# Per-step rstd on ScalarE and g folded into W1, in a kernel of sliding-window attention, LayerNorm and MLP

## Chip, cores and metric

The kernel runs on one core of a Trainium2 chip. The metric is the device time of one execution in microseconds.

The engines are TensorE (PE; its weight loads are PEld), VectorE (DVE), ScalarE (ACT), GpSimd (POOL) and SyncE (SP, which here only issues DMA). L191 is line 191 of the kernel that is spoken of. The line numbers of the two kernels differ.

## The reference, cut

```python
def _attn_ref(q, k, v):                      # 8 batches, 8 heads, 576 rows, head size 64
    ...
    rel = pos[:, None] - pos[None, :]
    mask = (rel >= 0) & (rel < 64)           # causal window of 64 rows
    scores = np.where(mask, scores, -1000000000.0)
    ...                                      # softmax
    return np.matmul(attn, v)

def _moe_ref(x, g_ln, w_ch1, w_ch2):         # x: (8, 576, 512)
    mu = np.mean(x, axis=-1, keepdims=True)
    var = np.mean((x - mu) ** 2, axis=-1, keepdims=True)
    xn = (x - mu) / np.sqrt(var + 1e-06) * g_ln
    ch = np.maximum(xn @ w_ch1, 0.0) @ w_ch2 # 512 -> 2048 -> 512
    return x + ch
```

The layer has no bias, and relu(s·a) = s·relu(a) for a positive s. So 1/sqrt(var + eps), called rstd, may be applied to each row before the first layer or only at the output. The gain g may be applied to the rows or to the rows of W1.

## The kernel before

The work is cut into nine groups of 512 rows. Groups 0 to 7 are the first 512 rows of the eight batches, and group 8 holds the last 64 rows of all eight (the tails, four blocks of two batches). While the MLP of group g runs on PE, the attention of group g+1 is computed in slots between its pieces. The schedule is written by hand: instructions of one engine run in the order of the program.

```python
    def w1_cast(i, eng):                     # W1 float32 -> float16, 128x1024 at a time
        ...
            nc.gpsimd.tensor_copy(out=dst, in_=t)

    def cast_qk(b, half):                    # q and k of a later group, on GpSimd
        ...

    def s_mask(g, j):                        # the mask is multiplied in on VectorE, in place
        pt = pts[(g, j)]
        ...
        nc.vector.tensor_tensor(out=ptv, in0=ptv, in1=mb, op=ALU.mult)

    def b_step(g, kb):                       # probabilities x values, then LayerNorm, 128 rows
        ...
        nc.vector.tensor_tensor(out=xn, in0=xps[:, :, 0:D], in1=rcp_b, op=ALU.mult)
        nc.vector.bn_stats(out=stats, in_=xn[...])
        nc.vector.bn_aggr(out=mvg[g][:, kb, :], in_=stats)
        nc.vector.scalar_tensor_tensor(      # z = (xn - mean) * g, not divided by the deviation
            out=z, in0=xn[...], scalar=mvg[g][:, kb, 0:1], in1=gB,
            op0=ALU.subtract, op1=ALU.mult)

    def group_stats(g, eng=nc.gpsimd):       # rstd of four blocks: integer guess, two Newton steps
        ...                                  # the guess on VectorE
        for _ in range(2):
            eng.tensor_tensor(out=ab, in0=rs, in1=rs, op=ALU.mult)
            eng.tensor_tensor(out=ab, in0=ab, in1=hv, op=ALU.mult)
            eng.tensor_scalar(out=ab, in0=ab, scalar1=-1.0, scalar2=1.5, op0=ALU.mult, op1=ALU.add)
            eng.tensor_tensor(out=rs, in0=rs, in1=ab, op=ALU.mult)

    def add_out(kb):                         # output = xn + rstd * ch
        nc.vector.scalar_tensor_tensor(
            out=o, in0=ch[kb], scalar=rstd[g][:, kb:kb + 1], in1=x_norm[(g, kb)][...],
            op0=ALU.mult, op1=ALU.add)
    ...
        if g > 0:
            at(4 if g == 1 else 0, group_stats, g)   # slot 0 of its own group
        ...
            at(2 + 6 * j, s_mask, b, j)              # slot 2: first mask product of group g+1
            ...
            at(e + 8, cast_qk, n, 0)                 # casts of group g+2, on the same GpSimd queue
```

The softmax here doesn't subtract the row's maximum and nothing guards it: scores larger than these inputs give would overflow.

## Time and profile before

| | before |
|---|---|
| time, median of 3 runs (lowest to highest) | 329.69 us (328.72 to 329.92) |
| span of the profiled run | 328.5 us |
| first Relu of group 2, an end mark of the prologue | 100.39 us |
| each of groups 2 to 5 | 32.2 us |
| groups 6 and 7 together | 67.3 us |
| last W2 cast begins | 47.20 us |

The group times are distances between the first Relu of one group and that of the next, read from the timeline. (The texts count a group from its first matmul, about 1 us earlier.)

First the table of engines and the chain of waits of the page. The engine table gives busy microseconds, share of the span, and instruction count.

```profile
PE 314.1 (96%) x2711; PEld 162.6 (49%) x2711; DVE 163.8 (50%) x307; ACT 155.4 (47%) x268; POOL 126.4 (38%) x230
...
PE 66%; DMA 13%; issue 8%; POOL 5%; SPq 4%; DVE 1%; ACT 1%; POOLq 0%; ACTq 0%
```

PE is the limit. The other engines have half their time free.

Next, groups of instructions. The columns are line, engine, operation, output from input, shape, count, then busy time in us and mean ns of one, then the idle time ahead of them and what ended it.

```profile
L321 DVE SCALAR_TENSOR_TENSOR z<-xn,mvg,gB 128x512 f16<-128x512 f32 x36 | 32.6, 907 | 1.3
L396 DVE SCALAR_TENSOR_TENSOR osb<-ch,rstdg,xn 128x512 f32<-128x512 f32 x36 | 27.0, 749 | 57.5 <-PE ch L387 46.1 <-issue 9.7 <-PE ch L426 1.6
...
L292 DVE TENSOR_TENSOR pt<-pt,mask 128x1024 f16<-128x1024 f16 x28 | 19.3, 690 | 20.9 <-ACT pt L285 11.9 <-ACT pt L279 9.0
...
L191 POOL CAST w1g<-w2s 128x1024 f16<-128x1024 f32 x4 | 4.2, 1062 | 1.5 <-DMA w2s<-in_moe_w_ch_dram 1.5
L191 POOL CAST w1g<-w1s 128x1024 f16<-128x1024 f32 x4 | 4.2, 1061 | 2.8 <-DMA w1s<-in_moe_w_ch_dram 2.6
```

The eight W1 casts are 8.4 us of GpSimd. The mask product is 690 ns on average, which matters below.

Then the timeline of GpSimd in the prologue (start, duration, engine, line, operation, output from input, count, and in brackets the idle time before and who ended it):

```profile
16.60 1.04 POOL L191 CAST w1g<-w1s 128x1024 f16<-128x1024 f32 x1 [0.73 <-DMA w1s<-in_moe_w_ch_dram]
...
27.60 1.04 POOL L191 CAST w1g<-w2s 128x1024 f16<-128x1024 f32 x1 [0.72 <-DMA w2s<-in_moe_w_ch_dram]
...
47.20 1.04 POOL L201 CAST w2s<-w2s 128x1024 f16<-128x1024 f32 x1 [0.38 <-DMA w2s<-in_moe_w_ch_dram]
```

The casts wait for DMA, not the other way round: there is some slack on GpSimd here. The waits of PE show where it stood still:

```profile
PE sc L275 <- DMA tkT<-tk: 2.2, 1, 2.2
PE ch L426 <- POOL w2s L201: 1.7, 2, 1.4
```

The first is the one late transpose of tail keys in group 7, the second the W2 casts of the prologue. Each line has the total, the number of times, and the longest.

Last, a steady group, as GpSimd and then as VectorE ran it:

```profile
101.13 0.18 POOL L352 TENSOR_SCALAR rstmp<-mvg 128x4 f32<-128x4 f32 x1
...
103.07 0.61 POOL L357 TENSOR_SCALAR rstmp<-rstmp 128x4 f32<-128x4 f32 x1
103.77 0.20 POOL L358 TENSOR_TENSOR rstdg<-rstdg,rstmp 128x4 f32<-128x4 f32 x1
103.90 1.04 POOL L128 CAST qk<-qk 128x1024 f16<-128x1024 f32 x1
```

### The profile page before, as it was taken

Reading aid. Unit: us, or ns where it says so; the run is one execution under the profiler, and the core shown is the slowest. Engines: PE = TensorE matmul, PEld = TensorE weight load, DVE = VectorE, ACT = ScalarE, POOL = GpSimd, SP = SyncE. Lnnn points to the kernel's source line nnn. Section 1 sums busy time; section 2 is a strip of 40 time slices with the busy share of each in tenths; the row PEclk is TensorE's granted clock in tenths of the full one; section 3 lists DMA queues with packets and bytes.
Section 4 is the critical chain, followed back from the end, with each engine's and each line's share of the span. In section 5 each row is a group of like instructions: output and inputs, shape, how many; then the busy total and the mean of one; then the engine's idle time right before and its main releaser. Section 6 shows DMA issues by size and latency. Waiting matters only on the chain.

```text
span 328.5 us, 6688 instructions
## 1 busy us (share of the span) xinstructions
PE 314.1 (96%) x2711; PEld 162.6 (49%) x2711; DVE 163.8 (50%) x307; ACT 155.4 (47%) x268; POOL 126.4 (38%) x230
## 2 busy tenths in 40 slices
PE   7989979999999999999999999999999999799993
PEld 2566435587654545454444444454445444344441
DVE  1895564584762564266526652655257713441021
ACT  2586504487636731682178217722772276216500
POOL 7566555648416501750184018301500462212000
PEclk9999989999999999999999999999999999999998
DMA  8999999976992898289938993991390397310022
GB/s 191 284 384 268 340 266 290 282 260 138 242 254 81 163 261 220 73 153 259 224 79 148 266 211 80 138 194 64 90 198 35 86 217 163 83 65 32 2 64 64
DMA packets 119329, 56.77 MB, mean 173 GB/s; under 512 B 95777, under 2 KB 112161, under 8 KB 119298
## 3 DMA queue, kind: packets, MB, share of 16 engines
q1 hardware_dynamic: 116096, 45.62, 60.2%
q0 software_dynamic: 3200, 10.72, 11.0%
q8 instruction: 21, 0.34, 0.4%
q14 instruction: 10, 0.08, 0.1%
q10 hardware_dynamic: 2, 0.00, 0.0%
HBM read 38.80 MB, written 9.44 MB: 147 GB/s over the span
## 4 chain that ended last, share of the span: by engine, by line
PE 66%; DMA 13%; issue 8%; POOL 5%; SPq 4%; DVE 1%; ACT 1%; POOLq 0%; ACTq 0%
PE ch L387 31%; PE hps L375 22%; DMA w2s<-in_moe_w_ch_dram 4%; DMA qk<-in_q_dram 4%; PE hph L411 4%; PE xps L307 3%; PE sc L275 2%; SPq L141 2%; PE ztp L332 2%; DMA w1s<-in_moe_w_ch_dram 2%; DMA tk<-in_k_dram 2%; DMA tv<-in_v_dram 1%; PE ch L426 1%; SPq L79 1%; PE tp L217 1%
## 5 line engine op out<-in xcount | busy, mean ns | idle before, releaser
L387 PE MATMUL ch<-w2s,hrT 128*128 128x512 f16 x544 | 125.0, 379 | 0.0
L375 PE MATMUL hps<-zT,w1g 128*128 128x512 f16 x480 | 109.9, 379 | 0.0
L379 ACT ACTIVATE hrT<-hps 128x512 f16<-128x512 f32 x120 | 72.0, 600 | 41.1 <-PE hps L375 40.6
L387 PEld LDWEIGHTS <-hrT 128*128 128x128 f16 x544 | 50.8, 98 | 56.4
L375 PEld LDWEIGHTS <-w1g 128*128 128x128 f16 x480 | 45.4, 98 | 54.6 <-issue 3.1
L366 POOL DMA_DIRECT2D out_dram<-osb x32 | 17.7, 554 | 130.9 <-DVE osb L396 59.4
L335 ACT COPY zT<-ztp 128x512 f16<-128x512 f16 x36 | 21.0, 583 | 77.7 <-PE ztp L332 77.5
L396 DVE SCALAR_TENSOR_TENSOR osb<-ch,rstdg,xn 128x512 f32<-128x512 f32 x36 | 27.0, 749 | 57.5 <-PE ch L387 46.1
L310 DVE RECIPROCAL rcp<-xps 128x8 f32<-128x8 f32 x36 | 7.4, 205 | 59.8 <-PE xps L307 59.8
L321 DVE SCALAR_TENSOR_TENSOR z<-xn,mvg,gB 128x512 f16<-128x512 f32 x36 | 32.6, 907 | 1.3
L292 DVE TENSOR_TENSOR pt<-pt,mask 128x1024 f16<-128x1024 f16 x28 | 19.3, 690 | 20.9 <-ACT pt L285 11.9
L128 POOL CAST qk<-qk 128x1024 f16<-128x1024 f32 x24 | 25.3, 1068 | 6.3 <-DMA qk<-in_q_dram 3.3
L285 ACT ACTIVATE pt<-sc 128x512 f16<-128x512 f32 x40 | 21.7, 596 | 12.1 <-PE sc L275 11.4
L315 DVE BATCH_NORM_STATS2 stats<-xn 128x6 f32<-128x512 f32 x36 | 25.0, 695 | 1.2
L313 DVE TENSOR_TENSOR xn<-xps,rcp 128x512 f32<-128x512 f32 x36 | 24.9, 692 | 1.2
L411 PE MATMUL hph<-zT,w1g 128*128 128x256 f16 x192 | 23.5, 273 | 1.5 <-ACT hrT L416 0.7
L411 PEld LDWEIGHTS <-w1g 128*128 128x128 f16 x192 | 18.0, 98 | 4.4 <-issue 1.8
L416 ACT ACTIVATE hrT<-hph 128x512 f16<-128x512 f32 x24 | 14.4, 599 | 10.2 <-PE hph L411 10.0
L147 POOL CAST vA<-v 128x512 f16<-128x512 f32 (+1 forms) x14 | 16.2, 1162 | 4.9 <-DMA v<-in_v_dram 4.6
L279 ACT ACTIVATE pt<-sc 128x512 f16<-128x512 f32 x32 | 17.4, 601 | 1.0
L307 PEld LDWEIGHTS <-pt 128*64 128x64 f16 x576 | 12.2, 110 | 9.2 <-issue 5.1
L209 ACT COPY qkT<-tp 128x1024 f16<-128x1024 f16 x10 | 10.0, 1012 | 11.4 <-PE tp L217 11.0
(65 smaller groups left out, 241.1 us busy)
## 6 DMA issues: line engine op xcount, KB each, us to landing
qk<-in_q_dram SPq DMA_DIRECT2D x16, 512.0 KB, 6.4
v<-in_v_dram SPq DMA_DIRECT2D x32, 256.0 KB, 5.8
out_dram<-osb POOLq DMA_DIRECT2D x32, 256.0 KB, 3.3
w2s<-in_moe_w_ch_dram SPq DMA_DIRECT2D x12, 512.0 KB, 5.9
qk<-in_k_dram SPq DMA_DIRECT2D x8, 512.0 KB, 6.9
qk<-in_k_dram SPq DMA_DIRECT2D x16, 256.0 KB, 5.8
w1s<-in_moe_w_ch_dram SPq DMA_DIRECT2D x4, 512.0 KB, 7.0
tk<-in_k_dram SPq DMA_DIRECT2D x8, 256.0 KB, 4.8
```

The costliest lines, as they stand in the source:

```text
L128: nc.gpsimd.tensor_copy(out=dst[:, :].rearrange("p (a j) e d -> p a e j d", j=j), in_=t[:, :].rearrange("p (a e j d) -> p a e j d", e=2, j ...
L285: nc.scalar.activation(out=pt[:, par], in_=sc[par], func=AF.Exp, bias=0.0, scale=scale)
L307: nc.tensor.matmul(out=xps[64 * r:64 * r + 64, h, :D + 1], lhsT=pt[:, par, hp, r, :], rhs=rhs, start=True, stop=True)
L313: nc.vector.tensor_tensor(out=xn, in0=xps[:, :, 0:D], in1=rcp_b, op=ALU.mult)
L315: nc.vector.bn_stats(out=stats, in_=xn[:, :, :].rearrange("p h d -> p (h d)"))
L321: nc.vector.scalar_tensor_tensor(out=z, in0=xn[:, :, :].rearrange("p h d -> p (h d)"), scalar=mvg[g][:, kb, 0:1], in1=gB, op0=ALU.subtract ...
L335: nc.scalar.copy(out=dst, in_=ztp)
L375: nc.tensor.matmul(out=hps, lhsT=w1g[:, kc, 128 * hc:128 * (hc + 1)], rhs=zT[g][:, kc, :], start=(kc == 0), stop=(kc == NKC - 1),)
L379: nc.scalar.activation(out=hrT[:, hc, :], in_=hps, func=AF.Relu, bias=0.0, scale=1.0)
L387: nc.tensor.matmul(out=ch[kb], lhsT=hrT[:, hc, 128 * kb:128 * (kb + 1)], rhs=w2s[:, hc, :], start=(hc == 0), stop=(hc == NHC - 1),)
L396: nc.vector.scalar_tensor_tensor(out=o, in0=ch[kb], scalar=rstd[g][:, kb:kb + 1], in1=x_norm[(g, kb)][:, :, :].rearrange("p h d -> p (h d) ...
L411: nc.tensor.matmul(out=hps[:, e], lhsT=w1g[:, kc, 128 * hc:128 * (hc + 1)], rhs=zT[g][:, kc, 256 * half:256 * half + 256], start=(kc == 0) ...
```

## The change

The intent: rows go to layer 1 fully normalised, so the output becomes a plain add and z needs no g. Rstd comes from two one-column ScalarE activations per block, exp(-0.5·ln(var + eps)), and the Newton chain goes. The gain is multiplied into W1 where W1 is cast anyway. Two smaller parts ride along: the tail blocks are loaded and cast some slots earlier, and their value tiles alternate between two buffer tags.

```diff
-    def w1_cast(i, eng):
+    def w1_cast(i):
...
-            nc.gpsimd.tensor_copy(out=dst, in_=t)
+        for c in range(2):
+            kc = 2 * pr + c
+            nc.gpsimd.tensor_scalar(
+                out=w1g[:, kc, (HID // 4) * q2:(HID // 4) * (q2 + 1)], in0=t[:, c],
+                scalar1=g4[:, kc:kc + 1], scalar2=None, op0=ALU.mult,
+            )
...
+    def r_step(g, kb):
+        rs = p_blk.tile([128, 1], FP32, tag="rs", name=f"rs_{g}_{kb}")
+        nc.scalar.activation(out=rs, in_=mvs[(g, kb)][:, 1:2], func=AF.Ln, bias=epst, scale=1.0)
+        nc.scalar.activation(out=rs, in_=rs, func=AF.Exp, bias=0.0, scale=-0.5)
+
+    def z_step(g, kb):
...
-        nc.vector.scalar_tensor_tensor(
-            out=z, in0=xn[...], scalar=mvg[g][:, kb, 0:1], in1=gB,
+        nc.vector.tensor_scalar(
+            out=z, in0=x_norm[(g, kb)][...], scalar1=mv[:, 0:1], scalar2=rs[:, 0:1],
             op0=ALU.subtract, op1=ALU.mult,
         )
...
-    def group_stats(g, eng=nc.gpsimd):      (all of it goes)
...
-            nc.vector.scalar_tensor_tensor(
-                out=o, in0=ch[kb], scalar=rstd[g][:, kb:kb + 1], in1=x_norm[(g, kb)][...],
-                op0=ALU.mult, op1=ALU.add)
+            nc.vector.tensor_tensor(out=o, in0=ch[kb], in1=x_norm[(g, kb)][...], op=ALU.add)
...
+    nc.scalar.preload_act_table_set("natural_log_exp_and_others")   # one set for Ln and Exp
-    nc.scalar.dma_start(out=g1, in_=...)    # g as one row of 2 KB, broadcast by PE
+    nc.scalar.dma_start(out=g4, in_=...)    # g as 512 elements of 4 bytes, one column per 128 rows
...
-        vt = p_va.tile(..., tag="vA", ...)
+        vt = p_va.tile(..., tag=("vA", "vB")[i % 2], ...)
...
     TAILS = { ... }                         # loads, casts and transposes of tails in earlier slots
```

More of the change, by code (lines that the diff above doesn't have):

```diff
@@ L12 @@
 FP16 = mybir.dt.float16
-I32 = mybir.dt.int32
-RSQRT_MAGIC = float(np.frombuffer(np.uint32(0x5F3759DF).tobytes(), dtype=np.float32)[0])
 AF = mybir.ActivationFunctionType
@@ L63 @@
     mbias = p_const.tile([128, 64], FP16, tag="mbias", name="mbias")
-    magt = p_const.tile([128, 4], FP32, tag="magt", name="magt")
-    gB = p_const.tile([128, DM], FP32, tag="gB", name="gB")
+    g4 = p_const.tile([128, NKC], FP32, tag="g4", name="g4")
+    epst = p_const.tile([128, 1], FP32, tag="epst", name="epst")
     w1g = p_const.tile([128, NKC, HID], FP16, tag="w1g", name="w1g")
@@ L71 @@
     qkT, vA, vB, pts = {}, {}, {}, {}
-    x_norm, zT, mvg, zsd, rstd = {}, {}, {}, {}, {}
+    x_norm, zT, zsd, mvs, rss = {}, {}, {}, {}, {}
     def load_qk(b, half):
@@ L110, in cast_tail @@
         k16 = p_in.tile([128, 2, H, D], FP16, tag="qk16_1", name=f"tk16_{i}")
-        vt = p_va.tile([128, 2, H, D + 1], FP16, tag="vA", name=f"vt_{i}")
+        vt = p_va.tile([128, 2, H, D + 1], FP16, tag=("vA", "vB")[i % 2], name=f"vt_{i}")
         tail16[i] = (q16, k16)
@@ L182, in w1_load @@
         )
-    def w1_cast(i, eng):
+    def w1_cast(i):
         q2, pr = divmod(i, 2)
         t = wst.pop(("w1", i))
-        dst = w1g[:, 2 * pr:2 * pr + 2, (HID // 4) * q2:(HID // 4) * (q2 + 1)]
-        if eng == "act":
-            nc.scalar.copy(out=dst, in_=t)
-        else:
-            nc.gpsimd.tensor_copy(out=dst, in_=t)
+        for c in range(2):
[4 more added lines that the diff above has]
+            )
     def w2_load(i):
@@ L315, in b_step @@
         nc.vector.bn_stats(out=stats, in_=xn[:, :, :].rearrange("p h d -> p (h d)"))
-        if g not in mvg:
-            mvg[g] = p_grp.tile([128, 4, 2], FP32, tag="mvg", name=f"mvg_{g}")
-        nc.vector.bn_aggr(out=mvg[g][:, kb, :], in_=stats)
-        z = p_blk.tile([128, DM], FP16, tag="z", name=f"z_{kblk}")
+        mv = p_blk.tile([128, 2], FP32, tag="mv", name=f"mv_{kblk}")
+        nc.vector.bn_aggr(out=mv, in_=stats)
+        mvs[(g, kb)] = mv
+    def r_step(g, kb):
+        rs = p_blk.tile([128, 1], FP32, tag="rs", name=f"rs_{g}_{kb}")
+        rss[(g, kb)] = rs
+        nc.scalar.activation(out=rs, in_=mvs[(g, kb)][:, 1:2], func=AF.Ln, bias=epst, scale=1.0)
+        nc.scalar.activation(out=rs, in_=rs, func=AF.Exp, bias=0.0, scale=-0.5)
+    def z_step(g, kb):
+        mv, rs = mvs.pop((g, kb)), rss.pop((g, kb))
+        z = p_blk.tile([128, DM], FP16, tag="z", name=f"z_{g}_{kb}")
         zsd[(g, kb)] = z
-        nc.vector.scalar_tensor_tensor(
-            out=z, in0=xn[:, :, :].rearrange("p h d -> p (h d)"), scalar=mvg[g][:, kb, 0:1], in1=gB,
+        nc.vector.tensor_scalar(
+            out=z, in0=x_norm[(g, kb)][:, :, :].rearrange("p h d -> p (h d)"), scalar1=mv[:, 0:1], scalar2=rs[:, 0:1],
             op0=ALU.subtract, op1=ALU.mult,
@@ L337, in zt_step @@
             nc.vector.tensor_copy(out=dst, in_=ztp)
-    def group_stats(g, eng=nc.gpsimd):
-        rstd[g] = p_grp.tile([128, 4], FP32, tag="rstdg", name=f"rstdg_{g}")
-        rs = rstd[g]
-        mv = mvg[g]
-        tmp = p_grp.tile([128, 3, 4], FP32, tag="rstmp", name=f"rstmp_{g}")
-        ve, hv, ab = tmp[:, 0], tmp[:, 1], tmp[:, 2]
-        nc.vector.tensor_scalar(out=ve, in0=mv[:, :, 1], scalar1=EPS, scalar2=None, op0=ALU.add)
-        nc.vector.tensor_scalar(
-            out=ab.bitcast(I32), in0=ve.bitcast(I32), scalar1=1, scalar2=None,
-            op0=ALU.logical_shift_right,
-        )
-        nc.vector.tensor_tensor(out=rs[:, :].bitcast(I32), in0=magt[:, :].bitcast(I32),
-                                in1=ab.bitcast(I32), op=ALU.subtract)
-        eng.tensor_scalar(out=hv, in0=mv[:, :, 1], scalar1=0.5, scalar2=0.5 * EPS,
-                                op0=ALU.mult, op1=ALU.add)
-        for _ in range(2):
-            eng.tensor_tensor(out=ab, in0=rs, in1=rs, op=ALU.mult)
-            eng.tensor_tensor(out=ab, in0=ab, in1=hv, op=ALU.mult)
-            eng.tensor_scalar(out=ab, in0=ab, scalar1=-1.0, scalar2=1.5, op0=ALU.mult, op1=ALU.add)
-            eng.tensor_tensor(out=rs, in0=rs, in1=ab, op=ALU.mult)
     stores, cur = [], [0]
@@ L395, in add_out @@
             o = p_blk.tile([128, DM], FP32, tag="osb", name=f"osb_{g}_{kb}", bufs=4)
-            nc.vector.scalar_tensor_tensor(
-                out=o, in0=ch[kb], scalar=rstd[g][:, kb:kb + 1],
-                in1=x_norm[(g, kb)][:, :, :].rearrange("p h d -> p (h d)"), op0=ALU.mult, op1=ALU.add,
+            nc.vector.tensor_tensor(
+                out=o, in0=ch[kb], in1=x_norm[(g, kb)][:, :, :].rearrange("p h d -> p (h d)"), op=ALU.add,
             )
@@ L444, in mlp_units @@
         return units
+    nc.scalar.preload_act_table_set("natural_log_exp_and_others")
     load_qk(0, 0)
     load_v(0, 0, 2)
-    g1 = p_const.tile([1, DM], FP32, tag="g1", name="g1")
-    ones1 = p_const.tile([1, 128], FP32, tag="ones1", name="ones1")
-    nc.scalar.dma_start(out=g1, in_=bass.AP(tensor=moe_g_ln.tensor, offset=moe_g_ln.offset, ap=[[DM, 1], [1, DM]]))
+    nc.scalar.dma_start(out=g4, in_=bass.AP(tensor=moe_g_ln.tensor, offset=moe_g_ln.offset, ap=[[1, 128], [128, NKC]]))
     load_qk(0, 1)
@@ L457 @@
     nc.vector.memset(mask, 1.0)
-    nc.vector.memset(magt, RSQRT_MAGIC)
-    nc.vector.memset(ones1, 1.0)
+    nc.vector.memset(epst, EPS)
     nc.gpsimd.affine_select(
@@ L479 @@
     for i in range(8):
-        w1_cast(i, "pool")
+        w1_cast(i)
     warm = ps_mm.tile([128, 512], FP32, tag="mm", name="warm")
@@ L492 @@
     keep_clock(4)
-    gps = ps_mm.tile([128, DM], FP32, tag="mm", name="gps")
-    nc.tensor.matmul(out=gps, lhsT=ones1, rhs=g1, start=True, stop=True)
-    nc.vector.tensor_copy(out=gB, in_=gps)
     keep_clock(1)
@@ L510 @@
     vB_cur(0, 2, 0)
+    r_step(0, 0)
+    z_step(0, 0)
     t_main(0, 0, 1, 0)
@@ L517 @@
     vB_prev(0, 2, 0)
+    r_step(0, 1)
+    z_step(0, 1)
     s_mm(0, 2, True)
@@ L522 @@
     zt_step(0, 1)
+    r_step(0, 2)
+    z_step(0, 2)
     s_mm(0, 3, True)
@@ L546 @@
     TAILS = {
-        6: ((1, load_tail, 0), (6, cast_tail, 0), (8, x_tail, 0), (16, s_mm, 8, 0), (17, s_mask, 8, 0),
-            (22, b_step, 8, 0), (28, zt_step, 8, 0),
-            (14, load_tail, 1), (24, cast_tail, 1), (26, x_tail, 1), (25, load_tail, 2), (30, cast_tail, 2)),
-        7: ((6, s_mm, 8, 1), (7, s_mask, 8, 1), (12, b_step, 8, 1), (17, zt_step, 8, 1),
-            (0, x_tail, 2), (12, s_mm, 8, 2), (13, s_mask, 8, 2), (18, b_step, 8, 2), (23, zt_step, 8, 2),
-            (7, load_tail, 3), (12, cast_tail, 3), (14, x_tail, 3), (18, s_mm, 8, 3), (19, s_mask, 8, 3),
-            (24, b_step, 8, 3), (29, zt_step, 8, 3)),
+        6: ((0, load_tail, 0), (3, cast_tail, 0), (5, x_tail, 0), (10, s_mm, 8, 0), (11, s_mask, 8, 0),
+            (16, b_step, 8, 0), (22, zt_step, 8, 0),
+            (10, load_tail, 1), (14, cast_tail, 1), (18, x_tail, 1), (20, load_tail, 2), (24, cast_tail, 2),
+            (26, x_tail, 2)),
+        7: ((1, s_mm, 8, 1), (2, s_mask, 8, 1), (7, b_step, 8, 1), (12, zt_step, 8, 1),
+            (7, s_mm, 8, 2), (8, s_mask, 8, 2), (13, b_step, 8, 2), (18, zt_step, 8, 2),
+            (0, load_tail, 3), (4, cast_tail, 3), (6, x_tail, 3), (13, s_mm, 8, 3), (14, s_mask, 8, 3),
+            (19, b_step, 8, 3), (24, zt_step, 8, 3)),
     }
@@ L560, in at, with bz @@
             slots[min(i, len(slots) - 1)].append((f, a))
+        def bz(i, *p):
+            at(i, b_step, *p)
+            at(i + 1, r_step, *p)
+            at(i + 2, z_step, *p)
         b = g + 1
         if g == 0:
-            at(0, b_step, 0, 3)
+            bz(0, 0, 3)
             at(1, zt_step, 0, 2)
             at(3, zt_step, 0, 3)
-            at(4, group_stats, 0, nc.vector)
             at(11, t_main, 1, 0, 0, 1)
@@ L575 @@
             at(17, s_mm, 1, 1, True)
-            at(18, b_step, 1, 0)
-            at(21, b_step, 1, 1)
+            bz(18, 1, 0)
+            bz(21, 1, 1)
             at(22, zt_step, 1, 0)
@@ L589 @@
             at(30, cast_qk, 2, 1)
-            at(31, b_step, 1, 2)
+            bz(31, 1, 2)
         if g == 1:
             at(0, alloc_qkT, 2)
-            at(1, b_step, 1, 3)
+            bz(1, 1, 3)
             at(2, zt_step, 1, 2)
@@ L613 @@
                 at(10 + 4 * j, s_mask, 2, j)
-                at(13 + 4 * j, b_step, 2, j)
+                bz(13 + 4 * j, 2, j)
                 at(17 + 4 * j, zt_step, 2, j)
@@ L619 @@
                 at(2 + 6 * j, s_mask, b, j)
-                at(7 + 6 * j, b_step, b, j)
+                bz(7 + 6 * j, b, j)
                 at(min(13 + 6 * j, 29), zt_step, b, j)
-        if g > 0:
-            at(4 if g == 1 else 0, group_stats, g)
         for i, f, *p in TAILS.get(g, ()):
-            at(i, f, *p)
+            if f is b_step:
+                bz(i, *p)
+            else:
+                at(i, f, *p)
         if 0 < g and b + 1 < B:
```

## The prediction

> **What bounds the kernel now.** TensorE. The engine table has PE busy 314.1 of 328.5 us; the chain of waits is 66% PE. In the timeline the middle groups repeat every 32.2 us (99.43, 131.66 ... 228.40 us) with PE gapless. VectorE (50%), ScalarE (47%) and GpSimd (38%) have room, so work saved there is worth nothing by itself. PE waits in two places:
> - Prologue, 0 to 49 us. DMA is about 90% busy. In the chain, w2 loads, then their GpSimd casts, release second-layer matmuls at 46.87 us (1.38 us gap before; 0.36 us at 44.09).
> - Group 7, 260.4 to 295.6 us, about 3 us longer than its neighbours. PE waits 2.19 us at 283.04 for transposed tail keys: tail 1's casts sat on GpSimd behind output stores until 256.9, so tail 2's v load started at 259.58, tail 3's loads at 269 to 275, its casts at 278.
>
> **Costs.**
> - Removed: integer and Newton steps, about 0.5 us VectorE and 2.7 us GpSimd a group; the g broadcast (2.07 us of PE, hidden). z loses its gB operand: 907 ns (749 undisturbed) becomes perhaps 450. The output add goes from 749 to about 695 ns, as the xn multiply (692).
> - Added: 72 one-column activations. Two ScalarE forms (583 ns for 512 columns, 1012 for 1024) leave about 155 ns fixed; the Trainium skill, "ScalarE: Activation LUTs", What ACT_TABLE_LOAD costs, adds about 93 ns for a pointer operand. Estimate 0.25 + 0.2 us. The same page has Ln and Exp in one set; the built program has one table load.
> - W1 cast: 8 casts of 1024 columns (1061 ns) become 16 multiplies of 512. A 512 cast takes 617 ns; the Trainium skill, "GPSIMD Engine Reference", Engine selection, calls one-input work "roughly line-rate". I estimate 0.65 to 0.95 us each: +2 to +6 us of GpSimd. No trace yet shows this operation at that size.
> - g load: 512 four-byte packets on the busy DMA: +0.3 to 0.9 us, from 27 ns mean packet time (60.2% of 16 engines over 116096 packets).
>
> **On the critical path.**
> - Steady groups: Ln waits for the aggregate, in front of the next Relu. At 107 to 110 us: aggregate ends 109.37, Ln and Exp about 109.9, Relu about 110.5 instead of 110.25, its PSUM buffer was wanted at 110.47. Stall under 0.1 us, once a group; layer 2 has none. About +0.5 us overall.
> - Prologue: GpSimd waits 3.4 us for DMA between the w1 casts and over 2 us after them, so most of its extra is absorbed; layer 1 of group 0 may start up to 1 us later (cast 3 ended 22.9, PE needed it at 22.84), swallowed by the w2 wait. Net +0.5 us.
> - Tails: casts now precede stores, vt alternates between two tags, tail 3 loads at slot 0: loads at 259, transposed by 272, wanted at about 274 us (estimates). The wait goes: -2.4 us.
>
> Net about -1.5 us: **328.2 us**, 8 in 10 between 325.8 and 331.5. Faster by over 2%: 2%; within: 91%; slower: 7%.
>
> **What would show it.** Right: groups of 32.2 to 32.4 us, PE gapless; no wait on tail keys; group 7 about 32.5 us; w2 casts still release near 47 us; W1 multiplies below 0.95 us; z below 0.6 us. Wrong: groups 0.5 us longer with PE waiting for Relu; W1 multiplies above 1.2 us and a later release; a new tail wait.
>
> **What would make it wrong.** A slow scalar-pointer multiply on GpSimd, dragging w2 casts and loads (+3 to 8 us); VectorE's faster z locking GpSimd out; several Relu stalls a group, 0.5 us times 14 or so.

## More of the kernel before

```profile
102.94 0.69 DVE L292 TENSOR_TENSOR pt<-pt,mask 128x1024 f16<-128x1024 f16 x1 [2.24 <-ACT pt L285]
```

The Newton steps fill GpSimd from 101.13 to 103.97 us, and the casts of q and k stand behind them. The first mask product of the group runs from 102.94 to 103.63, that is, before the casts begin. Nothing in the program asks for that order; it is how the queues happen to fall.

## The result, and the profile after

| | before | after |
|---|---|---|
| time, median of 4 runs (lowest to highest) | 329.21 us (328.27 to 329.92) | 340.97 us (340.13 to 343.05) |
| span of the profiled run | 328.5 us | 339.2 us |
| first Relu of group 2 | 100.39 us | 110.26 us |
| each of groups 2 to 5 | 32.2 us | 33.1 us |
| groups 6 and 7 together | 67.3 us | 64.7 us |
| last W2 cast begins | 47.20 us | 57.34 us |

The ratio is 1.0369 (95% interval 1.0313 to 1.0424): slower. A ratio in this document is the mean time of one kernel's runs over the mean of the other's runs of the same rounds, so it is not quite the ratio of the medians quoted beside it. Runs of different comparisons went to different chips, so between those I compare ratios to before. One hundredth in such a ratio is about 3.3 us.

The groups split the 10.7 us between the two profiled spans: +9.9 before group 2, +3.4 in groups 2 to 5 (about 0.86 each), -2.6 in groups 6 and 7, nothing worth naming after that.

The clock does play a part in the prologue. Both profiles are of runs with mean granted clocks of 0.992 and 0.995, but the clock is not even within them. In the profile of before, PE was granted half its clock from 46.90 to 50.30 us, and was busy all that time (stretch and length; busy time and count of PE, PEld, DVE, ACT and POOL; clock, DMA share, GB/s):

```profile
46.90:50.30 3.40, 3.40 (x12) 1.45 (x12) 2.06 (x4) 0.58 (x1) 2.08 (x2) 0.50 1.17 283
```

Half of 3.4 us is 1.7 us lost, an estimate. The timed runs bear it out: of the 25 runs of before in the three later sets of rounds, the 15 with a mean clock of 0.995 or more took 327.5 to 329.3 us, the 10 with 0.993 or less 329.8 to 331.5. The changed kernel's profile has a stretch of the same length, from 21.5 to 24.9 us. Why the clock was halved there is not shown. So differences of a microsecond or two before group 2, from one profile each, are not to be read without the clock. Against e3 and e9 below, which have the prologue of before and full clock in it (group 2 at 98.95 and 98.15 us), the changed kernel, its own stretch included, loses 11.3 to 12.1 us before group 2, not 9.9.

The engines and the chain of the page after:

```profile
PE 313.9 (93%) x2709; PEld 162.0 (48%) x2709; DVE 163.7 (48%) x269; ACT 170.8 (50%) x340; POOL 124.6 (37%) x166
...
PE 72%; POOL 7%; DVE 7%; DMA 6%; SPq 3%; ACT 2%; issue 1%; POOLq 0%
PE ch L374 35%; PE hps L362 23%; DVE pt L291 6%; POOL w1g L187 5%; DMA w2s<-in_moe_w_ch_dram 4%; PE hph L397 4%; PE xps L306 3%; PE sc L274 3%; PE ztp L340 2%; SPq L139 2%; DMA w1s<-in_moe_w_ch_dram 2%; POOL w2s L200 1%; PE tp L216 1%; SPq L77 1%; ACT pt L278 1%
```

PE has the same work, and VectorE and GpSimd are busy about as long as before, yet the span grew. Totals do not tell it; the chain does. Two lines are named in it now that were not before: the mask product on VectorE (L291, 6%) and the W1 multiplies on GpSimd (L187, 5%). The groups of instructions show both:

```profile
L291 DVE TENSOR_TENSOR pt<-pt,mask 128x1024 f16<-128x1024 f16 x28 | 36.1, 1291 | 18.2 <-ACT pt L278 10.9 <-ACT pt L284 7.4
...
L383 DVE TENSOR_TENSOR osb<-ch,xn 128x512 f32<-128x512 f32 x36 | 24.8, 689 | 65.1 <-PE ch L374 64.0 <-PE ch L412 1.1
L329 DVE TENSOR_SCALAR z<-xn,mv,rs 128x512 f16<-128x512 f32 x36 | 21.8, 607 | 4.7 <-ACT rs L323 4.3
...
L187 POOL TENSOR_SCALAR w1g<-w1s,g 128x512 f16<-128x512 f32 x8 | 12.7, 1598 | 1.0 <-DMA w1s<-in_moe_w_ch_dram 1.0
L187 POOL TENSOR_SCALAR w1g<-w2s,g 128x512 f16<-128x512 f32 x8 | 12.3, 1557 | 0.0
L322 ACT ACTIVATE rs<-mv,epst 128x1 f32<-128x1 f32 x36 | 10.6, 295 | 26.5 <-DVE mv L316 26.5
...
L323 ACT ACTIVATE rs<-rs 128x1 f32<-128x1 f32 x36 | 7.3, 203 | 1.1
```

The multiplies take 1.6 us each and 25.0 us together, against the 8.4 us of the casts they replace. The mask product, which nobody touched, went from 690 to 1291 ns on average.

GpSimd in the prologue:

```profile
17.44 12.68 POOL L187 TENSOR_SCALAR w1g<-w1s,g 128x512 f16<-128x512 f32 x8 [0.98 <-DMA w1s<-in_moe_w_ch_dram]
30.10 12.34 POOL L187 TENSOR_SCALAR w1g<-w2s,g 128x512 f16<-128x512 f32 x8
...
57.34 1.04 POOL L200 CAST w2s<-w2s 128x1024 f16<-128x1024 f32 x1 [1.44 <-DMA w2s<-in_moe_w_ch_dram]
```

The brackets that held waits for DMA between the casts are gone: GpSimd is now the one that others wait for, the multiplies end at 42.4 instead of 28.6 us, and the W2 casts end 10 us later. The waits of PE agree:

```profile
PE hph L397 <- POOL w1g L187: 2.9, 3, 1.4
PE xps L306 <- DVE pt L291: 2.8, 4, 0.7
```

The tail keys are no longer in this list. The second line is new: once in each of four groups PE waits 0.7 us for the mask product. A steady group shows why, on GpSimd, VectorE and PE in turn:

```profile
144.02 1.05 POOL L126 CAST qk<-qk 128x1024 f16<-128x1024 f32 x1
145.00 1.05 POOL L123 CAST qk<-qk 128x1024 f16<-128x1024 f32 x1
...
148.25 1.88 POOL L145 CAST vA<-v 128x2048 f16<-128x2048 f32 x1
```

```profile
145.91 4.78 DVE L291 TENSOR_TENSOR pt<-pt,mask 128x1024 f16<-128x1024 f16 x1 [2.72 <-ACT pt L278]
```

```profile
144.54 5.49 PE L362 MATMUL hps<-zT,w1g 128*128 128x512 f16 x24
150.74 0.22 PE L306 MATMUL xps<-vB,pt 128*64 128x65 f16 x1 [0.71 <-DVE pt L291]
```

Without Newton steps ahead of them, the casts of q and k start right after the output store. They are under way when the mask product is released, and the product, 0.69 us of work, ends at 150.69, just after the last cast of the train (150.13). PE needed it at 150.03. The Trainium skill, "SBUF — State Buffer", Who interferes with whom, says that a VectorE instruction with two inputs from SBUF contends with a GpSimd instruction that reads SBUF. The mask product has two such inputs; the z of the new form has one.

### The profile page after: what moved, and what is told of

It is laid out like the page before. It is cut to its first block, busy times and chain, and to the rows that moved or that the text cites. A ratio compares the mean times of both kernels' runs of the same rounds, so it can differ in the third digit from the quotient of the medians. Undisturbed runs are those within 1.5% of the kernel's fastest.

```text
span 339.2 us, 6653 instructions
## 1 busy us (share of the span) xinstructions
PE 313.9 (93%) x2709; PEld 162.0 (48%) x2709; DVE 163.7 (48%) x269; ACT 170.8 (50%) x340; POOL 124.6 (37%) x166
## 4 chain that ended last, share of the span: by engine, by line
PE 72%; POOL 7%; DVE 7%; DMA 6%; SPq 3%; ACT 2%; issue 1%; POOLq 0%
PE ch L374 35%; PE hps L362 23%; DVE pt L291 6%; POOL w1g L187 5%; DMA w2s<-in_moe_w_ch_dram 4%; PE hph L397 4%; PE xps L306 3%; PE sc L274 3%; PE ztp L340 2%; SPq L139 2%; DMA w1s<-in_moe_w_ch_dram 2%; POOL w2s L200 1%; PE tp L216 1%; SPq L77 1%; ACT pt L278 1%
## 5 line engine op out<-in xcount | busy, mean ns | idle before, releaser
L383 DVE TENSOR_TENSOR osb<-ch,xn 128x512 f32<-128x512 f32 x36 | 24.8, 689 | 65.1 <-PE ch L374 64.0
L291 DVE TENSOR_TENSOR pt<-pt,mask 128x1024 f16<-128x1024 f16 x28 | 36.1, 1291 | 18.2 <-ACT pt L278 10.9
L397 PE MATMUL hph<-zT,w1g 128*128 128x256 f16 x192 | 24.9, 278 | 4.5 <-POOL w1g L187 2.9
L126 POOL CAST qk<-qk 128x1024 f16<-128x1024 f32 x24 | 24.9, 1043 | 8.6 <-DMA qk<-in_k_dram 4.8
L312 DVE TENSOR_TENSOR xn<-xps,rcp 128x512 f32<-128x512 f32 x36 | 24.9, 691 | 1.2
L329 DVE TENSOR_SCALAR z<-xn,mv,rs 128x512 f16<-128x512 f32 x36 | 21.8, 607 | 4.7 <-ACT rs L323 4.3
L322 ACT ACTIVATE rs<-mv,epst 128x1 f32<-128x1 f32 x36 | 10.6, 295 | 26.5 <-DVE mv L316 26.5
L210 DVE COPY qkT<-tp 128x1024 f16<-128x1024 f16 x6 | 7.3, 1219 | 27.4 <-PE tp L216 27.3
L278 ACT ACTIVATE pt<-sc 128x512 f16<-128x512 f32 x32 | 17.4, 601 | 3.3 <-PE sc L274 2.7
```

The costliest lines, as they stand in the source:

```text
L126: nc.gpsimd.tensor_copy(out=dst[:, :].rearrange("p (a j) e d -> p a e j d", j=j), in_=t[:, :].rearrange("p (a e j d) -> p a e j d", e=2, j ...
L329: nc.vector.tensor_scalar(out=z, in0=x_norm[(g, kb)][:, :, :].rearrange("p h d -> p (h d)"), scalar1=mv[:, 0:1], scalar2=rs[:, 0:1], op0=A ...
L383: nc.vector.tensor_tensor(out=o, in0=ch[kb], in1=x_norm[(g, kb)][:, :, :].rearrange("p h d -> p (h d)"), op=ALU.add,)
L397: nc.tensor.matmul(out=hps[:, e], lhsT=w1g[:, kc, 128 * hc:128 * (hc + 1)], rhs=zT[g][:, kc, 256 * half:256 * half + 256], start=(kc == 0) ...
```

## The experiments

My theory after reading the two profiles had four parts: (1) the W1 multiply at 1.58 us delays the prologue; (2) the casts, freed of the Newton steps, hold the mask product; (3) the g load and the Ln and Exp in the ScalarE queue cost the prologue a little; (4) the earlier tails give back about 2.5 us. The rivals were that Ln and Exp stall the Relus in every group (for 2), and that DMA luck makes the late prologue (for 1).

Edits are against the changed kernel unless said otherwise. e5, e6 and e8 are built on e1 and, like it, leave g out. Their outputs are wrong, which doesn't matter for the times.

### e1: the W1 multiply undone

```diff
-        for c in range(2):
-            nc.gpsimd.tensor_scalar(out=w1g[...], in0=t[:, c], scalar1=g4[:, kc:kc + 1], ...)
+        nc.gpsimd.tensor_copy(out=dst, in_=t)
```

> The changed kernel with one thing undone: W1 is cast plainly on GpSimd (8 casts of 1024 columns) and g is not applied, so the result is wrong on purpose. The four-byte g load, Ln and Exp per step and the rest stay. In the changed kernel the 16 multiplies took 25.0 us of GpSimd and group 2 began at 109.4 us instead of 99.4. Theory A (the multiply on GpSimd alone delays the prologue): casts back to about 1.05 us each, group 2 begins at 99.5 to 101 us, time about 331 us (-10). Rival B (Ln and Exp in the ScalarE queue, or the g load, delay the prologue): group 2 begins at 105 us or later and the time stays above 336. In both, groups 2 to 5 stay at 33.1 us with a 4.8 us mask multiply.

Measured: 333.66 us (333.49 to 334.88), ratio 1.0136 (1.0085 to 1.0187), with the relative error of 0.47 that leaving g out must give. Group 2 begins at 102.83 instead of 110.26 us, and groups 2 to 5 stay at 33.1 us. So the multiply is worth 0.0233 of the ratio, about 7.6 us with some 2.5 us of uncertainty from the two intervals (the two profiled spans differ by 7.4), all of it in the prologue, and the groups' 0.86 us has another cause. The time is 2.7 us above what I expected: 2.4 us of prologue are left over against before, and 3.9 against e3, whose profile has full clock there.

The left-over is partly visible in the ScalarE queue of e1's prologue:

```profile
20.45 0.30 ACT L318 ACTIVATE rs<-mv,epst 128x1 f32<-128x1 f32 x1 [0.47 <-DVE mv L312]
20.78 0.20 ACT L319 ACTIVATE rs<-rs 128x1 f32<-128x1 f32 x1
20.89 1.07 ACT L280 ACTIVATE pt<-sc 128x512 f16<-128x512 f32 x2
```

ScalarE idles 0.47 us until the statistics come, and the exponentials of the next block, which PE waits for, stand behind Ln and Exp. The first cast of q began at 6.01 us, against 5.05 in before: the 512 four-byte elements of g delay the first loads.

### e2: the casts kept behind the first mask product

```diff
+    def hold_pool(g, j):                    # one column of GpSimd that reads the masked tile
+        nc.gpsimd.tensor_copy(out=h, in_=held.pop((g, j))[:, 0, 0, 0, 0:1])
...
                 at(2 + 6 * j, s_mask, b, j)
+                if j == 0:
+                    at(3, hold_pool, b, j)
```

> The changed kernel plus one one-column GpSimd copy per group (from group 2 on) that reads the first masked score tile, so that GpSimd's casts of the next q, k, v begin only when that mask multiply is over. Theory A (the mask multiply on VectorE is held off by the train of GpSimd casts, which the removed Newton steps used to keep out of the way): mask multiply of block 0 back from 4.8 to 0.7 us, groups 2 to 5 back from 33.1 to about 32.3 us, time about 337.5 (-3.4). Rival B (Ln and Exp before the Relu on ScalarE lengthen the groups): groups stay at 33.0 or more and the time within 1 us of 341.

Measured: correct, 337.71 us (336.36 to 339.76), ratio 1.0261 (1.0187 to 1.0335). The groups are 32.32 to 32.34 us. VectorE and GpSimd in the same place of the group:

```profile
144.77 0.69 DVE L294 TENSOR_TENSOR pt<-pt,mask 128x1024 f16<-128x1024 f16 x1 [2.72 <-ACT pt L278]
```

```profile
145.53 0.19 POOL L298 COPY hold<-pt 128x1 f16<-128x1 f16 x1 [2.64 <-DVE pt L294]
145.65 1.04 POOL L126 CAST qk<-qk 128x1024 f16<-128x1024 f32 x1
```

Putting the casts behind the product gives back 0.77 of the 0.86 us a group with Ln and Exp still in place. The rival (Relu stalls) is left with at most 0.1 us a group, which is what the prediction gave it.

### e3: before, with the new tails alone

```diff
-        vt = p_va.tile(..., tag="vA", ...)
+        vt = p_va.tile(..., tag=("vA", "vB")[i % 2], ...)
-    TAILS = { old slots }
+    TAILS = { new slots }
```

> The kernel before with only the tails' new slots and the value tile of the tails alternating between two tags. Theory: the 2.2 us wait of TensorE for the transposed tail keys goes; groups 6 and 7 together fall from 67.3 to about 64.7 us; time about 326.8 us (-2.5), everything else as before. If the tails gained only because of what else changed (GpSimd free of Newton steps), the two groups stay above 66 us.

Measured, against before: correct, 326.05 us (325.48 to 327.89), ratio 0.9907 (0.9851 to 0.9962). Groups 6 and 7 take 64.7 us instead of 67.3. That part of the change is a gain of its own, and the prediction had it.

### e4: before, with the Newton steps moved to VectorE

```diff
-            at(4 if g == 1 else 0, group_stats, g)
+            at(4 if g == 1 else 0, group_stats, g, nc.vector)
```

This is the opposite test of the casts' role: it frees GpSimd of the Newton steps and adds no Ln, no Exp and no new z.

> The kernel before with one thing changed: the Newton steps of groups 1 to 8 run on VectorE instead of GpSimd. No Ln or Exp, no g multiply. Theory A (Newton steps on GpSimd delayed its casts past the mask multiply): casts now start about 3 us earlier in each of groups 2 to 5, the mask multiply of block 0 goes from 0.7 to about 4.8 us, these groups from 32.2 to about 33.1 us, time about 333 (+3.4). Rival B (longer groups come from Ln and Exp): groups stay at 32.2 to 32.4 us, time 329 to 330.

Measured, against before: correct, 341.34 us (339.51 to 342.29), ratio 1.0355 (1.0294 to 1.0415). I expected 333, so the form was missed: here the instruction held is not the mask product but the Newton product ahead of it. VectorE, then GpSimd:

```profile
133.98 6.47 DVE L355 TENSOR_TENSOR rstmp<-rstdg 128x4 f32<-128x4 f32 x1
...
141.82 0.68 DVE L292 TENSOR_TENSOR pt<-pt,mask 128x1024 f16<-128x1024 f16 x1
```

```profile
134.30 1.05 POOL L128 CAST qk<-qk 128x1024 f16<-128x1024 f32 x1
...
140.37 0.52 POOL L151 MEMSET vB<- 64x520 f16 x1
```

A product of 128x4 elements, 0.16 us when undisturbed (141.15 in the same group), lasts 6.47 us, to the end of the casts. Groups 2 to 5 grow to 34.6 us, one of them to 36.2; in that one PE was granted half its clock for 3.4 us (144.0 to 147.4), which accounts for the 1.7 us more. So casts that come early cost the group even where nothing else of the change is present. The collision is shown twice, by taking it away (e2) and by bringing it into before (e4), where it holds another product and for longer.

### m1: single instructions measured

Single instructions and trains of four were put into group 8, where time does not matter. One run, correct.

> The changed kernel plus a row of single instructions in group 8, where GpSimd and VectorE have nothing else: each form once, one engine at a time. If the per-partition multiply is slow by itself: 1.5 to 1.6 us for 512 columns on an idle chip, as in the prologue. If it was slow there because VectorE held the memory port: 0.65 to 0.9 us here. The immediate form shows whether the scalar's pointer or the operation costs (pointer: about 0.65 us; operation: about 1.55 us). The float32 cast of 512 is the yardstick: 0.62 us. Then three trains of four GpSimd instructions of 1024 columns with one VectorE instruction released by the instruction ahead of them. If VectorE's second SBUF input waits for the whole train of GpSimd reads: the tensor-tensor multiply (0.68 us alone) takes about 4 us beside four casts, and 0.7 us beside four memsets, which only write; the tensor-scalar multiply (no second tensor) takes under 1.5 us beside casts, or the casts stretch.

Forms on GpSimd, in the groups of instructions:

```profile
L549 POOL TENSOR_SCALAR bO<-bA,g 128x512 f16<-128x512 f32 x1 | 1.6, 1567 | 0.0
...
L554 POOL TENSOR_TENSOR bT<-bA,g 128x512 f16<-128x512 f32 x1 | 1.0, 1028 | 0.0
...
L548 POOL CAST bO<-bA 128x512 f16<-128x512 f32 x1 | 0.6, 622 | 0.0
```

The multiply by a per-partition pointer takes 1.57 us here too, away from the prologue and its DMA. It is not the pointer: an immediate scalar took 1.48 us, float16 input 1.55, float32 output 1.55, and 1024 columns 2.83. It is the multiply by a scalar on this engine. The two-input product with g broadcast along the row, which computes the same, takes 1.03 us. On VectorE the pointer multiply took 0.49 us.

For the trains I expected a product beside casts to last about 4 us. It lasted 1.42 us beside four casts and 0.68 beside four memsets, which read nothing:

```profile
323.10 1.42 DVE L575 TENSOR_TENSOR bV<-bB 128x1024 f16<-128x1024 f16 x1
...
327.61 0.68 DVE L575 TENSOR_TENSOR bV<-bB 128x1024 f16<-128x1024 f16 x1
```

A VectorE multiply with one input took 1.15 us beside four casts; alone it was not measured at that size. That GpSimd's reads are what collides agrees with the page cited above; the length of the hold in the kernel was missed.

### e5, e6 and e8: what is left in the prologue

e5 is e1 with g loaded as one row. e6 is e1 with the Ln, Exp and z of the prologue issued behind the exponentials of the next block. e8 is e1 with both of these and the hold of e2.

```diff
# e5
-    nc.scalar.dma_start(out=g4, in_=... 512 elements of 4 bytes)
+    nc.scalar.dma_start(out=g1, in_=... one row of 2 KB)
# e6, and alike for the other blocks
+    s_mm(0, 2, True)
     r_step(0, 1)
     z_step(0, 1)
-    s_mm(0, 2, True)
```

> The run with the plain W1 cast, and g loaded as one row of 2 KB as in the kernel before instead of 512 elements of four bytes (g unused, result wrong on purpose). If the small packets delay the first loads: the first GpSimd cast of q begins at 5.0 us instead of 6.0, and the time falls by about 1 us, to 332.7. If not: the first cast stays at about 6.0 us and the time within 0.5 us of 333.7.

> The run with the plain W1 cast, and in the prologue the Ln, Exp and z of block kb issued behind the next block's score exponentials or statistics instead of ahead of them (result wrong only for lack of g). If Ln waiting for the aggregate holds the score exponentials in ScalarE's queue and so stretches each of the first blocks from 3.0 to 3.9 us: the first full-width layer-1 matmul of group 0 moves from 34.5 to about 31.5 us, the time falls by about 2.5 us, to 331. If the prologue is bound by DMA alone: the matmul may move but the time stays within 0.7 us of 333.7.

> All three together on the plain W1 cast: casts held behind the first mask multiply, row load of g, Ln and Exp later in the prologue (result wrong for lack of g). If the causes found add up: 333.7 minus 3.4, 1 and 2.5, about 327, within 1 us of the kernel before with the new tails (326.05), so that nothing else of the change costs more than about 1 us. If it stays above 329, a cause is missing.

Measured, all against before: e5 331.94 us (331.61 to 335.52), ratio 1.0137 (1.0060 to 1.0213); e6 332.15 us (331.71 to 333.09), ratio 1.0114 (1.0070 to 1.0158); e8 328.36 us (328.28 to 329.89), ratio 1.0006 (0.9960 to 1.0052). Before was 327.98 us in these rounds.

In e5 the first q cast begins at 5.03 instead of 6.01 us, so the four-byte load does cost the start 1 us, but the ratio is that of e1: the time does not show it. In e6 the first full-width layer-1 matmul moves from 34.47 to 31.92 us, nearly the 31.5 expected, but the gain of 0.002 lies inside its interval, so the expected 2.5 us did not reach the end. Neither is resolved alone. (In the profiles group 2 begins at 101.31 us in e5 and 101.68 in e6, against 102.83 in e1; e6 has full clock there, the other two a stretch of 3.4 us at half clock.) Together with the hold, e8 gains 0.013 over e1, about 4.3 us; by the groups (32.33 us) the hold is 3.1 us of it, which leaves about 1 us for the other two.

e8 has the new tails and should then stand near e3. It is 0.0099 above, about 3.3 us with 2.4 of uncertainty from the two intervals; the profiled spans differ by 2.2 us, and in both the clock is full until the last 3 us. Of the 2.2, 0.4 are the groups' Ln and Exp and 1.76 lie before group 2 (100.71 us, against 98.95 in e3). Most of these are there when layer 1 begins, as the timeline of PE in e8 shows:

```profile
22.10 1.03 PE L400 MATMUL hph<-zT,w1g 128*128 128x256 f16 x8 [1.64 <-ACT zT L346]
```

In e3 this first matmul of layer 1 starts at 20.82 us, and the first full-width one at 30.03 instead of 31.48. In e8 the z of block 1 waits 1.24 us for Ln and Exp, and the copy of its transpose then stands behind the exponentials of block 2 on ScalarE; in e3 z needs no rstd. So in the prologue, normalising the rows before layer 1 is on PE's path. This is read from the two profiles; no run tested it alone. The remaining 1.1 us of the 3.3 are in no profile.

### m2, m3 and m4: how long a product is held

The trains of m1 held a product 1.4 us and the kernel 4.8. These three kernels, one run each and all correct, tried what makes the difference: waits between the casts and the length of the train (m2), the casts' access pattern and the kernel's own sequence of casts (m3), the single source of the casts and the form of the product (m4).

```diff
# m4, in group 8; mk is the kernel's own mask product, tt a plain product
+        train(1, four, tt)                  # four casts of one source
+        train(2, [... two sources ...] * 2, mk)
+        train(3, four, mk)
+        train(4, four, t4)                  # t4: a product of 128x4
```

> The changed kernel plus trains of GpSimd casts of 1024 columns in group 8, each with one VectorE tensor-tensor multiply of 1024 columns (0.69 us alone) released just ahead of it. In the first measurement, where each cast had to wait for the end of the cast before, the multiply took 1.42 us, not the 4 us I expected; in the changed kernel it took 4.8 us beside casts issued back to back. If the read port passes to VectorE only where GpSimd has a gap between instructions: about 4.3 us beside 4 casts and 6.3 us beside 6 casts issued without waits, 1.2 to 1.5 us beside 4 casts that wait for each other. If the length of the train does not matter: about 1.4 us in all three, and the 4.8 us has another cause.

> One look; result correct. In group 8, four trains of GpSimd instructions without waits between them, each beside one VectorE product with two operands from SBUF, issued as the train starts: (1) four contiguous 128x1024 casts beside the mask product in the kernel's own form (in place, mask broadcast); (2) four casts in the kernel's permuted 4-D form beside a plain 128x1024 product; (3) the kernel's own sequence (permuted cast, flat cast, small memset, permuted cast, flat cast, small memset, cast of V to a stride of 65) beside the mask product; (4) four contiguous casts that alternate between two sources beside a plain product. Theory A (the form of the mask product lets GpSimd go first each time): trains 1 and 3 hold the product 4 to 6 us, 2 and 4 about 1.4. Theory B (the permuted casts do it): 2 and 3 hold it 3 to 6 us, 1 and 4 about 1.4. Theory C (only the kernel's mixture does): 3 alone, about 5 us. If all four read about 1.4 us, the holding depends on something else, such as the instant of the release, and stays open.

> One look; result correct. m3 held the mask product 4.3 us beside four casts of one source tile (train 1) but 1.4 us beside the kernel's sequence, and a plain product 1.4 us beside permuted casts and casts of two alternating sources. Here: (1) four casts of one source beside a plain product; (2) four casts of alternating sources beside the mask product; (3) m3's train 1 again, casts of one source beside the mask product; (4) casts of one source beside a product of 128x4. If the one source does it: 1, 3 (and perhaps 4) about 4.3 us, 2 about 1.4. If the mask product's form is needed with some casts: 2 and 3 about 4.3, 1 about 1.4. If the outcome only hangs on the instant at which the product asks: train 3 need not repeat its 4.3 us, and the long ones fall anywhere; then the length of a hold stays open, and only the collision is shown.

Measured. m2: 1.41 us in all three trains; its theory, that length and waits decide, fell. m3: 4.33 us in train 1 (mask form, casts of one source), 1.41 in the other three, the kernel's own sequence among them. m4: 4.33 in train 1 (plain product, casts of one source), 1.41 in trains 2 and 3, 0.88 in train 4. VectorE and GpSimd of m4:

```profile
322.81 4.33 DVE L557 TENSOR_TENSOR bV<-bB 128x1024 f16<-128x1024 f16 x1
...
332.21 1.41 DVE L559 TENSOR_TENSOR bV<-bV,mask 128x1024 f16<-128x1024 f16 x1
```

```profile
324.58 2.01 POOL L553 CAST bF<-bA 128x1024 f16<-128x1024 f32 x2
...
332.04 2.48 POOL L553 CAST bO<-bA 128x1024 f16<-128x1024 f32 x2
```

The first product waits until the last cast (326.59) is over and no cast is stretched; the second goes in after the cast under way, and the next cast pays for it (2.48 us for two instead of 2.02). m4's train 3 is the very pair that m3's train 1 held 4.33 us, and it was held 1.41. So neither the product's form nor the source, pattern or mixture of the casts decides. What does stays open. The instant of asking is a candidate: the two long holds began 0.19 us after their first cast, the short ones of m2, m3 and m4 0.16 to 0.18 us after, but no run varied that alone, and both long ones were also the first train of their run. For the kernel it is enough that the outcome is steady there: in all nine profiles whose casts are not held back, the product of each of the four groups asked 0.91 us after the start of a cast of 1.05 us and lasted 4.77 to 4.79 us.

### f1 and f2: repairs

f1 only replaces the form of the multiply. f2 adds the hold of e2, the order of e6, and loads g as four rows of 512 bytes that PE turns.

```diff
# f1
-            nc.gpsimd.tensor_scalar(out=..., in0=t[:, c], scalar1=g4[:, kc:kc + 1], ...)
+            gb = ... g4[:, kc:kc + 1] with stride 0 over 512 columns
+            nc.gpsimd.tensor_tensor(out=..., in0=t[:, c], in1=gb, op=ALU.mult)
```

> The changed kernel with one thing changed: g multiplied into W1 on GpSimd as a tensor-tensor multiply with g read as a broadcast second tensor (1.03 us for 512 columns in the idle measurement) in place of the scalar form (1.57 us). Right result. 16 of them: about 16.5 us of GpSimd instead of 25.0, group 2 begins about 5 us earlier, time about 336. If only the number of GpSimd instructions or the g load counted: no change.

> The changed kernel with every cause found repaired and a right result: broadcast multiply for W1, g loaded as four rows of 512 bytes and turned on TensorE, Ln and Exp later in the prologue's ScalarE queue, casts held behind the first mask multiply. The same with a plain cast and no g took 328.4; 16.5 us of GpSimd instead of 8.4 in the prologue should cost 1 to 3 us more: about 330. It should not beat the kernel before with the new tails.

Measured, both correct, before 329.27 us in these rounds: f1 334.11 us (332.88 to 334.25), ratio 1.0137 (1.0094 to 1.0180). f2 329.77 us (328.19 to 331.12), ratio 1.0014 (0.9971 to 1.0057). f1's multiplies are 16.8 us of GpSimd, twice the casts of before, and yet its ratio is that of e1, where they are plain casts, and its group 2 begins at 103.44 us against 102.83 in e1. I had expected 336 us. So the slack of the prologue does take up 8 us more, within the 2 us that the intervals allow; it does not take up 17. f2 is level with before: the repaired change is not worth making, since e3 has its only gain.

### e9: the best version again

The kernel of e3, in five rounds, beside f1 and f2.

> The kernel before with the new tail schedule once more, on the same chip as the repaired change: ratio to the kernel before 0.99, about 326 us, and faster than the repaired change by 3 us or more.

Measured, against before: correct, 325.50 us (325.16 to 326.92), ratio 0.9892 (0.9862 to 0.9922). It beats before by 1.1%, which is clear of the noise, and f2 of the same rounds by 4 us. The groups of its profile explain 2.6 us of about 3.6. The rest lies before group 2 (98.15 us against 100.39 in the one profile of before), in code that the two kernels share. What differs there is the clock: the 3.4 us at half clock in the profile of before account for about 1.7 of these 2.2 us. In the timed runs 5 of 6 of e9, but only 6 of 11 of before, had a mean clock of 0.995 or more; among those alone the means are 325.4 and 328.6 us, 3.1 apart.

## Why the prediction was wrong

It said 328.2 us with 325.8 to 331.5 as its range and gave slower 7%. The time was 340.97.

**The term that was mis-sized: the W1 multiply.** The prediction had "0.65 to 0.95 us each: +2 to +6 us of GpSimd". It rested on a 512 cast of 617 ns and on the Trainium skill, "GPSIMD Engine Reference", Engine selection: "1-input is roughly line-rate". The trace has 1.58 us and +16.6 us. At the predicted size the step after it, "most of its extra is absorbed", would have held, as f1 shows: +8 us of GpSimd were absorbed. At +16.6 the multiplies became the chain (GpSimd ran without a gap from 17.4 to 42.4 us, where it had waited for DMA before), and about 7.6 us reached the end (e1). Its own list of what would make it wrong had this case at "+3 to 8 us", the right size, but the estimate had been taken from another operation and was trusted.

**The step that failed: "work saved there is worth nothing by itself".** The prediction counted the removed Newton steps as free time on an engine with room. They also held the casts of q and k back until the mask product was through. Without them the casts hold the product 4.8 us, and PE waits 0.7 us in each of four groups; e2 takes back 0.77 us a group, about 3.1 us in all, and e4 brings the collision into before. It did name contention of the two engines, but in the wrong direction, VectorE's z shutting out GpSimd.

**The prologue's small terms.** "Net +0.5 us" was too low also without the multiply. The g load costs 1 us at the start of the first cast, near the "0.3 to 0.9" given for it. That and Ln and Exp ahead of the exponentials are about 1 us together, measured only in combination. The prediction also counted Ln and Exp against the Relus of the steady groups alone and let layer 1 of group 0 start late for the W1 casts only. In the prologue they stand before z, and so before layer 1, as the profiles of e8 and e3 show: of the 3.3 us between these two, 0.4 are Ln and Exp in the groups, about 1.8 lie before group 2, most of it at the start of layer 1, and 1.1 stay unexplained.

**What was right.** The tails: the wait on tail keys is gone, and groups 6 and 7 gained 2.6 us for the predicted 2.4. Ln and Exp in a steady group: 0.1 us for "under 0.1". Their durations: 295 and 203 ns for 0.25 + 0.2 us. The Trainium skill, "ScalarE: Activation LUTs", What ACT_TABLE_LOAD costs, gave that estimate its 93 ns for a pointer operand and agrees: Ln, whose bias is one, takes 92 ns more than Exp, which has none. The output add: 689 ns for 695. z only nearly: 607 ns for "below 0.6" and for the 450 of the cost table; a pass without disturbance takes about 550. That the wait on tail keys would go came from the right mechanism, as e3 shows, not from luck.

The sum, in us: +7.6 multiply, +3.1 held mask product, about +1 g load and queue order, +3.3 between e8 and e3, -3.1 tails and what came with them in e3 (the clock among it). That is 11.9, against the 12.1 of the ratio 1.0369. The agreement proves nothing: but for the split of the second and third term these are differences along one chain of ratios (changed kernel, e1, e8, e3, before), which add up by construction.

## What to carry to other kernels

An instruction that costs nothing by its busy time can still be what keeps two others apart; before removing one from a queue, look at what stands behind it, when that will now start, and what it will then run beside on an engine that shares ports with it. Do not size an operation by a cheaper one of the same shape on the same engine: have it measured alone, or take the form that was. And try the parts of a bundled change one by one: here the smallest part, the order of the tail loads, was the only gain.

## What the Trainium skill lacked or had wrong

- "GPSIMD Engine Reference", Engine selection, calls one-input elementwise work "roughly line-rate" and two-input work about twice as slow as on VectorE. Here a 128x512 cast takes 0.62 us, but a multiply by a scalar 1.57 (pointer) or 1.48 us (immediate), against 0.49 on VectorE; the two-input product with a broadcast operand takes only 1.03. The page lacks the scalar forms, and for them the order of one and two inputs is the other way round.
- "SBUF — State Buffer", SBUF: two separate sides, says that whoever starts first has the shared ports "for the whole instruction". That GpSimd's reads and not its writes collide agrees (1.42 us beside casts, 0.68 beside memsets). But a product can be held through several GpSimd instructions: 4.78 us through a train of casts in the kernel, 6.47 us for a 128x4 product in e4, and in m3 and m4 the same pair gave 4.33 us once and 1.41 us once. The page does not say who is served next when a train follows.
- "ScalarE: Activation LUTs", What ACT_TABLE_LOAD costs: about 93 ns for a pointer operand; the runs show 295 ns with one and 203 ns without, 92 apart. Nothing to correct.
